# Attention and two mixture layers in one kernel: unit 1's decay summed by VectorE in the keys' tile, remainders of the head on GpSimd, fillers, bank and a load re-placed

## The chip, the cores and the metric

One core of a Trainium2 chip runs the whole program. The metric is the device time of one execution in microseconds (us), taken as the median of several runs; a profile is one further execution. TensorE (PE in rows) does the matmuls, VectorE (DVE), ScalarE (ACT) and GpSimd (POOL) the rest; SyncE (SP) only issues DMAs, and ScalarE and GpSimd issue DMAs of their own as well.

## The reference

Inputs are float32; w_in and w_out reach the kernel as float64, and are converted on the chip.

```python
# B, H, S, D = 2, 8, 576, 64
scores = (1 / sqrt(D)) * matmul(q, k.transpose(0, 1, 3, 2))
cum = cumsum(maximum(s, 0), axis=-1)
bias = -(cum[:, :, :, None] - cum[:, :, None, :])
scores = where(causal, -1e9, scores + minimum(bias, 0))
attn = exp(scores - max(scores)); attn /= attn.sum(-1) + 1e-9
x = matmul(attn, v)                      # -> 1152 tokens x 512
h = x @ w_in; x = maximum(0.01 * h, h) @ w_out          # d_ff 2048
p = domain_probs / domain_probs.sum(-1)                 # 4 experts
out = sum(p[:, e] * (maximum(x @ w1[e], 0) @ w2[e]) for e in range(4))
```

## The kernel before

The work on attention is cut into units. A unit is two heads of one batch over a stretch of tokens: units 0 to 7 are the first 256 tokens (two query tiles i = 1, 0 of 128, two heads j, so four items each), units 8 to 15 the other 320. The function attention() walks over all items in one list; at step i it does the scores of item i, the exponentials of item i-1, the transposes of item i-3, the products with the values of item i-5 and the unit's finish at i-7, and yields three times. The loop at the foot of the program (`for at_ in range(3*64)`, "the head") drives it, and puts other work between: filler matmuls, sums of the decay, the conversion of weights and, from i=24, the first pieces of the dense layer. The head ends when eight units are done. The order on every engine is the order of this program text (`fixed = True`), nothing is moved by a scheduler. DMAs that SP and ScalarE issue take eight completion counters (DMAHW0 to DMAHW7) in turn, in the order of the program, and an issue waits until the DMA eight places before it on the same counter has landed.

The causal decay enters as an additional row of the keys: row D=64 of the tile k_e[n % 3] (ke in rows) holds cum of the unit's two heads, and q_e (qe) has ones there. For unit 0 VectorE computes that row itself: `own` holds the two rows of s on partition 64, and a scan (TENSOR_TENSOR_SCAN in the trace, SCALAR_TENSOR_TENSOR in the listings of order) writes the sums into ke. For later units the scans of all sixteen heads on partitions 0 to 15 (pos, cum; function sums, first 256 columns and then the rest) are computed, and decay(n) issues a DMA on SP that carries two rows of cum into ke. For units 8 and up the float32 keys come again into kd, 288 KB, by a DMA that GpSimd issues, and the rows from cum_d in DRAM.

A score tile is a matmul (ps_sc) that VectorE masks and reduces in one operation (z, mn); ScalarE takes the exponential, TensorE transposes (ps_pt), ScalarE copies (pv), TensorE multiplies with the values (ps_o). Each unit of units 0 to 7 takes the one buffer of ps_o, 256 of 512 columns; VectorE divides by the row sums out of it (xo), TensorE transposes (ps_x).

Weights: fetch64(n) has ScalarE issue a load of 1024 KB of float64 (r); supply() turns it into a float32 tile raw in five steps (one on ScalarE, four on VectorE), has ScalarE store it, issue the next load, round it (w, first half) and another engine compute the remainder `w lo` = raw - w (second half). CONVERTING names the steps i at which supply() goes one step on; from i=31 on it does so in every step. idling(n) is n matmuls that write to the bank `nothing`, read by no one; they stand in each step between the transposes and the products. A float32 matmul is two records in the trace, so that one filler is "x2" there and a single row in a listing of the order.

Of the kernel before, what the change touches and what calls it, by code (L numbers as in the profile page):

```python
# [9 lines left out]
F32 = mybir.dt.float32  # L10
F32R = mybir.dt.float32r
# [8 lines left out]
def attention_moe_moe2(ctx: ExitStack, tc: tile.TileContext, q, k, v, s, w_in, w_out, probs, w1, w2, out):  # L20
# [54 lines left out]
    def f32(ap):  # L75
        return ap.bitcast(F32)
# [35 lines left out]
    def fetch64(n):  # L112
        src, (rows, _) = stream[n][:2]
        r64 = r64p.tile([P, 1024, 2], U32, tag="r64", name="r64")
        r64s.append(r64)
        nc.scalar.dma_start(r64.rearrange("p (a b) t -> p a (b t)", a=rows), src)
# [113 lines left out]
    def split_steps(raw, shape):  # L230

        w = wpool.tile([P, 2, 1024], F32R, tag="w", name="w")
        nc.scalar.copy(w[:, 0], raw)
        yield
        (nc.vector if fixed else nc.gpsimd).tensor_tensor(w[:, 1], raw, f32(w[:, 0]), ALU.subtract)
        yield w.rearrange("p l (a b) -> p l a b", a=shape[0])

    def up_piece(e, f, c):
# [283 lines left out]
    def cumulative():  # L522


        nonlocal cum, idle
        pos, zero, cum = (early.tile([BH, S], F32, name=n) for n in ("pos", "zero", "cum"))
        cum2, own = early.tile([BH, 2, S], F32R, name="cum2"), early.tile([P, 2, half[0]], F32, name="own")[D : D + 1]
        idle = early.tile([P, half[0]], F32, name="idle")

        def sums(lo, hi):  # L530
            part = slice(lo, hi)
            nc.vector.tensor_scalar(pos[:, part], pos[:, part], 0.0, D ** 0.5, ALU.max, ALU.mult)
            nc.vector.tensor_tensor_scan(cum[:, part], pos[:, part], zero[:, part], cum[:, lo - 1 : lo] if lo else 0.0, ALU.add, ALU.add)

        nc.sync.dma_start(own, s[:2, : half[0]])
        nc.scalar.dma_start(pos, s)
        nc.vector.memset(idle, 0.0)
        nc.vector.memset(zero, 0.0)
        idling(8)
        load_keys(0, nc.scalar)  # L540
        load_keys(1, nc.scalar)
        nc.vector.tensor_scalar(own, own, 0.0, D ** 0.5, ALU.max, ALU.mult)
        for j in range(2):
            nc.vector.tensor_tensor_scan(k_e[0][D : D + 1, j], own[:, j], idle[D : D + 1], 0.0, ALU.add, ALU.add)
        load_values(0, nc.scalar)
        fetch64(0)
        sums(0, half[0])
        decay(1, k_e[1])
        load_values(1)
        yield  # L550
        sums(half[0], S)
        yield
        nc.scalar.copy(cum2[:, 0], cum)
        yield
        nc.vector.tensor_tensor(cum2[:, 1], cum, f32(cum2[:, 0]), ALU.subtract)
        nc.sync.dma_start(cum_d.rearrange("l h k -> h l k"), f32(cum2))
        yield
# [104 lines left out]
    class Unit:  # L662
# [3 lines left out]
        def __init__(self, n):  # L666
            b, hp, i0, i1 = self.of = of_unit(n)
            self.items = [(i, j) for i in reversed(range(i0, i1)) for j in range(2)]
            self.ks, self.kd, self.qs = k_split.pop(n) if i0 else (None, k_e[n % 3], q_e[n % 3])
            self.vs = v_s[n % 4]  # L670
            self.z, self.mn, self.pv = {}, {}, {}
            self.o = self.xo = self.rest = None

# [25 lines left out]
        def transposes(self, i, j):  # L699
            z = self.z.pop((i, j))  # L700
            pv = self.pv[i, j] = ap.tile([P, QT, P], F32, tag="pv", name="pv", bufs=4)[:, : i + 1]
            for k0 in range(0, i + 1, 4):
# [3 lines left out]
                    nc.tensor.transpose(pt[:, (kt - k0) * P : (kt - k0 + 1) * P], z[:, tiles[kt][0] : tiles[kt][2]], ident)  # L706
                nc.scalar.copy(pv[:, k0:k1].rearrange("p t q -> p (t q)"), pt)

        def values(self, i, j):
            b, hp, i0, i1 = self.of  # L710
            if self.o is None:
                self.o = ps_o.tile([P, 512], F32, tag="o", name="ps_o")[:, : (i1 - i0) * (2 * D + 2)].rearrange("p (t c) -> p t c", t=i1 - i0)
            pv, cols = self.pv.pop((i, j)), slice(j * (D + 1), (j + 1) * (D + 1))
            for kt in range(i + 1):
                nc.tensor.matmul(self.o[:, i - i0, cols], pv[:, kt], self.vs[:, kt, cols], start=(kt == 0), stop=(kt == i))
            if (i, j) == (i0, 1):
                st = ap.tile([P, i1 - i0, 2, 1], F32, tag="st", name="st")
                sums = self.o[:, :, 0 :: 2 * D + 1].rearrange("p t (h c) -> p t h c", c=1)
                nc.vector.tensor_scalar(st, sums, 1e-9, None, ALU.add)
                nc.vector.reciprocal(st, st)  # L720
                self.xo = ap.tile([P, i1 - i0, 2, D], F32, tag="xo", name="xo", bufs=2)
                o = self.o[:, :, 1 : 2 * D + 1].rearrange("p t (h c) -> p t h c", h=2)
                nc.vector.tensor_tensor(self.xo, o, st.to_broadcast([P, i1 - i0, 2, D]), ALU.mult)

        def finish(self, i, j):

            nonlocal done
            b, hp, i0, i1 = self.of
            if (i, j) != (i0, 1):
                return  # L730
            base, q0, q1 = tiles[i0][:2] + tiles[i1 - 1][2:]
            x = ps_t.tile([P, 512], F32, tag="pt", name="ps_x")[:, : q1 - base]
            for i in reversed(range(i0, i1)):
                nc.tensor.transpose(x[:, tiles[i][0] - base : tiles[i][2] - base], self.xo[:, i - i0].rearrange("p h c -> p (h c)"), ident)
            c = int(i0 > 0)
            dst = slice(b * half[c], (b + 1) * half[c])
            if c == 0:
                nc.scalar.copy(x_t[0][:, 0, hp, dst], x)
                self.rest = x, hp, dst
            else:  # L740
                nc.scalar.copy(x_t[1][:, hp, dst], x)
                done += 1
# [5 lines left out]
                nc.vector.tensor_tensor(x_t[0][:, 1, hp, dst], x, f32(x_t[0][:, 0, hp, dst]), ALU.subtract)  # L748
                done += 1

    done = 0
    ending = False


# [2 lines left out]
    def attention():  # L757

        nonlocal ending
        items, starts, n = [], {}, 0  # L760
        i, split = 0, iter(())
        while n < units or i < len(items) + 8:
            if n < units and i == len(items):
                u = Unit(n)
                starts[n] = i
                items += [(u, *of) for of in u.items]
                if n + 2 < units and not 0 <= n + 2 - 2 * NP < 2:
                    load_keys(n + 2)
                    if n + 2 < 2 * NP:
                        decay(n + 2, k_e[(n + 2) % 3])  # L770
                if n in (2 * NP - 4, 2 * NP - 2):
                    load_keys(n + 4 if n == 2 * NP - 4 else n + 3)
                n += 1
            if n < units - 1 and i == starts[n - 1] + 2:
                load_values(n + 1)
            if i == starts[n - 1] and 2 * NP <= n < units:
                split = split_keys(n)
            for step, lag in STEPS:
                if 0 <= i - lag < len(items):
                    u, *of = items[i - lag]  # L780
                    step(u, *of)
                if lag == 1:
                    next(split, None)
                if lag in (1, 3, 7):

                    late = i - 5 + (lag == 7)
                    ending = lag != 3 and 0 <= late < len(items) and items[late][1:] == items[late][0].items[-1]
                    yield i
            i += 1
# [9 lines left out]
    with ExitStack() as phase:  # L799
# [3 lines left out]

        OPENED = (24, 25, 26, 27, 28, 29, 31, 33, 35)

        CONVERTING = (*range(5, 16), *range(17, 31, 2))
        side, units_of_w, late, opened = attention(), supply(), late_splits(), 0
        nothing = ps_mm.tile([P, 512], F32, tag="mm", name="nothing")
        with tc.tile_pool(name="early", bufs=1) as early:
            ones = pads(early)  # L810
            sums = cumulative()
            next(sums)
            main = mlps(phases[0])

            for at_ in range(3 * 64):
                i = next(side)
                if done == 2 * NP and at_ % 3 == 2:
                    break
                if at_ % 3 == 0 and i in (6, 8):
                    nc.scalar.copy(q_s[i // 2 - 3][D:DK, 1], ones[D:DK])  # L820
                if at_ % 3 == 1:
                    if i < 18:
                        idling(2 if i < 6 else 1)
                    elif opened < len(OPENED) and i >= OPENED[opened] and opened < 3 * (done // 2):
                        next(main)
                        opened += 1
                if at_ % 3 < 2 and i >= 31:
                    onto_held()
                if at_ % 3 == 2:
                    if i == 3:  # L830
                        fetch64(1)
                    if i in (3, 4, 5):
                        next(sums)
                    if i in CONVERTING or i >= 31:
                        next(units_of_w)
        hidden_pool(phase, 6)
# [92 lines left out]
```

## Time and profile before

| | |
|---|---|
| median of 3 runs | 726.74 us (726.07 to 726.77) |
| the profiled execution's own time | 725.75 us |
| its span, first to last instruction | 723.9 us (1.85 us of the time lie around it) |
| busy: TensorE, VectorE, ScalarE, GpSimd | 707.4, 442.2, 322.4, 253.6 us |
| granted TensorE clock, mean | 0.999 |
| bytes moved by DMA | 70.68 MB |
| instructions | 11398 |

Busy times are sums over the whole span; in the first 60 us the engines share the work differently from later, so the rows below are read by stretch. One difference between two kernels is the difference of their medians; the profiled execution lies 0.99 us below the median.

### The profile page before, as it was taken

The page shows a single profiled execution, that of the slowest core. Times are in us where ns is not written, and L with a number is a line of the kernel's source. Part 1 is how long each engine was busy: PE and PEld are TensorE (multiplying, and loading weights), DVE is VectorE, ACT ScalarE, POOL GpSimd, SP SyncE. Part 2 cuts the span into 40 slices and gives each one's busy share as a digit, 9 for nine tenths or more (in the row PEclk, how much of TensorE's full clock was granted, in tenths as well). Part 3 has the DMA queues.
Part 4 walks back from the last instruction along what each step waited for, and adds up shares of the span by engine and source line. Part 5 has one row for each costly group of instructions (what it writes and reads, how often), then busy time and mean ns, then how long its engine had stood idle before and what let it go on. Part 6 is the DMA issues. An engine that isn't in the chain of part 4 may idle for free.

```text
span 723.9 us, 11398 instructions
## 1 busy us (share of the span) xinstructions
PE 707.4 (98%) x4376; PEld 644.8 (89%) x4376; DVE 442.2 (61%) x893; ACT 322.4 (45%) x642; POOL 253.6 (35%) x226
## 2 busy tenths in 40 slices
PE   8899999999999999999999999999999999999998
PEld 7678889888878999999988989889889898898986
DVE  6778897998679656844943644545346344364452
ACT  5667877876735755634432322314224133232210
POOL 5000000000028789883372442704625227142200
PEclk9999999999999999999999999999999999999999
DMA  8966868575452222221120302101111021020002
GB/s 220 238 190 170 233 177 249 174 239 211 159 184 88 86 90 88 73 75 59 39 79 1 88 30 59 59 1 59 58 32 56 30 59 59 0 59 1 1 35 97
DMA packets 41878, 70.68 MB, mean 98 GB/s; under 512 B 4112, under 2 KB 23328, under 8 KB 41824
## 3 DMA queue, kind: packets, MB, share of 16 engines
q1 hardware_dynamic: 31296, 41.87, 19.6%
q10 hardware_dynamic: 9376, 25.73, 10.6%
q0 software_dynamic: 1152, 2.36, 1.6%
q8 instruction: 34, 0.56, 0.3%
q14 instruction: 20, 0.16, 0.1%
HBM read 59.11 MB, written 10.82 MB: 97 GB/s over the span
## 4 chain that ended last, share of the span: by engine, by line
PE 91%; DVE 3%; ACT 2%; DMA 2%; issue 1%; ACTq 0%; DVEq 0%; SPq 0%
PE ps_d L43 41%; PE ps_u L43 36%; PE ps_o L43 6%; PE ps_sc L43 4%; PE ps_pt L43 3%; DMA r<-in_moe_w_in_dram 1%; DMA ke<-in_k_dram 1%; PE nothing L43 1%; DVE t L43 1%; ACT z L43 1%; ACT w L43 0%; DVE w L43 0%; PE ps_x L43 0%; ACT pv L43 0%; DVE z L43 0%
## 5 line engine op out<-in xcount | busy, mean ns | idle before, releaser
L43 PE MATMUL ps_u<-t,w 128*128 128x320 f32 (+1 forms) x1680 | 236.5, 299 | 1.2 <-DVE t L43 1.2
L43 PEld LDWEIGHTS ps_u<-t,w 128*128 128x128 f32 x1680 | 233.0, 189 | 4.8 <-DVE t L43 1.4
L43 PE MATMUL ps_d<-w,ht 128*128 128x512 f32 (+1 forms) x876 | 203.4, 388 | 0.0
L43 PEld LDWEIGHTS ps_d<-w,ht 128*128 128x128 f32 x876 | 160.9, 188 | 31.5
L43 POOL TENSOR_TENSOR w<-raw,w 128x512 fp32r<-128x512 f32 (+2 forms) x72 | 109.1, 1535 | 218.6 <-ACT w L43 218.5
L43 ACT ACTIVATE ht<-ps_u 128x320 fp32r<-128x320 f32 (+2 forms) x176 | 74.2, 432 | 161.9 <-DVE ps_u L43 129.3
L43 DVE SCALAR_TENSOR_TENSOR oacc<-ps_d,pn,oacc 128x512 f32<-128x512 f32 (+1 forms) x64 | 47.5, 743 | 104.0 <-PE ps_d L43 104.0
L43 PE MATMUL ps_d<-ht,w 128*128 128x320 f32 (+1 forms) x576 | 109.5, 340 | 1.3 <-DVE y L43 1.3
L43 ACT CAST w<-raw 128x1024 fp32r<-128x1024 f32 (+2 forms) x88 | 63.9, 757 | 82.4 <-PE ps_d L43 76.4
L43 PEld LDWEIGHTS ps_d<-ht,w 128*128 128x128 f32 x576 | 90.9, 188 | 7.2 <-issue 1.7
L43 PEld LDWEIGHTS ps_o<-vs,pv 128*128 128x128 f32 x480 | 63.1, 191 | 8.7 <-issue 3.8
L43 DVE SCALAR_TENSOR_TENSOR ht<-ps_u,ht 128x320 fp32r<-128x320 f32 (+1 forms) x128 | 56.4, 453 | 23.3 <-ACT ht L43 22.0
L43 DVE TENSOR_TENSOR ps_u<-ps_u,tmp 128x320 f32<-128x320 f32 (+1 forms) x120 | 56.2, 471 | 23.5 <-PE ps_u L43 21.9
L43 PE MATMUL ps_o<-vs,pv 128*128 128x65 f32 x480 | 62.9, 267 | 3.0 <-issue 1.3
L43 POOL TENSOR_TENSOR w<-sums,w 128x1024 fp32r<-128x1024 f32 x24 | 58.7, 2445 | 8.0 <-ACT w L43 8.0
L43 DVE TENSOR_TENSOR tmp<-ps_u,tmp 128x320 f32<-128x320 f32 (+1 forms) x80 | 36.9, 464 | 39.7 <-PE ps_u L43 38.7
L43 POOL TENSOR_TENSOR sums<-raw 128x256 f32<-128x256 f32 x48 | 37.3, 797 | 58.9 <-DVE sums L43 57.4
L43 PE MATMUL ps_u<-x,w 128*128 128x512 f32 x192 | 56.6, 411 | 0.9 <-DVE x L43 0.9
L43 ACT ACTIVATE z<-z,mn 128x256 f32<-128x256 f32 (+4 forms) x80 | 48.5, 607 | 20.0 <-DVE mn L43 13.6
L43 POOL DMA_DIRECT2D kd<-in_k_dram x8 | 5.1, 638 | 140.6 <-PE ps_sc L43 140.6
L43 DVE CUSTOM_DVE_ANT_0 z<-ps_sc,mask 128x256 f32<-128x256 f32 (+4 forms) x80 | 41.0, 513 | 15.4 <-PE ps_sc L43 12.1
L43 ACT COPY pv<-ps_pt 128x512 f32<-128x512 f32 (+3 forms) x96 | 38.9, 422 | 14.1 <-PE ps_pt L43 13.7
(77 smaller groups left out, 657.2 us busy)
## 6 DMA issues: line engine op xcount, KB each, us to landing
raw<-in_moe_w_dram SPq DMA_DIRECT2D x32, 512.0 KB, 3.5
raw<-w_f SPq DMA_DIRECT2D x24, 512.0 KB, 3.9
r<-in_moe_w_in_dram ACTq DMA_DIRECT2D x8, 1024.0 KB, 6.3
w_f<-raw ACTq DMA_DIRECT2D x16, 512.0 KB, 3.8
r<-in_moe_w_out_dram ACTq DMA_DIRECT2D x8, 1024.0 KB, 7.6
qr<-in_q_dram SPq DMA_DIRECT2D x16, 160.0 KB, 7.6
kd<-in_k_dram POOLq DMA_DIRECT2D x8, 288.0 KB, 6.3
kr<-in_k_dram SPq DMA_DIRECT2D x8, 288.0 KB, 3.6
```

The lines of the kernel that those rows point to most:

```text
L43: ins = call(*args, **kw)
```

## The change

Five things are edited. Unit 1 gets its decay like unit 0: `own` has four rows, a second DMA brings the s of unit 1, and VectorE scans them into k_e[1] between the first score tiles; the decay DMA of unit 1 goes, that of unit 2 is issued behind the key loads of unit 3, and the common sums are computed later. In the head the remainders of the weights are computed by GpSimd. Units 0 to 7 share one ps_o buffer, even units in its last columns and odd ones in its first, with the tiles' places mirrored in odd ones. The second float64 load is issued at i=4 in place of 3. The table CONVERTING and the fillers are re-placed: two fillers in steps 12 to 23 (before, one in 12 to 17 and none in 18 to 23).

```diff
-        (nc.vector if fixed else nc.gpsimd).tensor_tensor(w[:, 1], raw, f32(w[:, 0]), ALU.subtract)
+        (nc.vector if fixed and not heading else nc.gpsimd).tensor_tensor(w[:, 1], raw, f32(w[:, 0]), ALU.subtract)
...
-        nc.sync.dma_start(own, s[:2, : half[0]])
+        for n in range(2):
+            nc.sync.dma_start(own[:, 2 * n : 2 * n + 2], s[n * H : n * H + 2, : half[0]])
...
-        for j in range(2):
-            nc.vector.tensor_tensor_scan(k_e[0][D : D + 1, j], own[:, j], idle[D : D + 1], 0.0, ALU.add, ALU.add)
         load_values(0, nc.scalar)
         fetch64(0)
+        load_values(1)
+        for j in range(4):
+            nc.vector.tensor_tensor_scan(k_e[j // 2][D : D + 1, j % 2], own[:, j], idle[D : D + 1], 0.0, ALU.add, ALU.add)
+            if j > 0:
+                yield
         sums(0, half[0])
-        decay(1, k_e[1])
-        load_values(1)
         yield
...
+        def slot(self, i):
+            i0, i1 = self.of[2:]
+            return i - i0 if i0 > 0 or self.even else i1 - 1 - i
...
+                    if shared_o is None:
+                        shared_o = ps_o.tile([P, 512], F32, tag="o", name="ps_o")
+                    o = shared_o[:, 512 - n :] if self.even else shared_o[:, :n]
...
                     load_keys(n + 2)
-                    if n + 2 < 2 * NP:
-                        decay(n + 2, k_e[(n + 2) % 3])
+
+                    for m in () if n == 0 else (2, 3) if n == 1 else range(n + 2, min(n + 3, 2 * NP)):
+                        decay(m, k_e[m % 3])
...
-        CONVERTING = (*range(5, 16), *range(17, 31, 2))
+        CONVERTING = (*range(5, 10), *range(12, 22), *range(23, 31, 2))
...
-                    if i < 18:
-                        idling(2 if i < 6 else 1)
+                    if i < 24:
+                        idling(2 if i < 6 or i >= 12 else 1)
...
-                    if i == 3:
+                    if i == 4:
                         fetch64(1)
-                    if i in (3, 4, 5):
-                        next(sums)
+                    if i < 7:
+                        next(sums, None)
```

VectorE at the start of the program, the difference of the two orders (ISA z,mn is the masking operation of one score tile, ISA mn the read of its minimum; ke_113 is the keys' tile of unit 0, ke_115 that of unit 1):

```order
-L43 TENSOR_SCALAR own<-own 1x512
+L43 TENSOR_SCALAR own<-own 1x1024
 L43 SCALAR_TENSOR_TENSOR ke_113<-own,idle 1x256 x2
+L43 ISA z,mn<-ps_sc,mask 128x256
+L43 ISA mn 128x1
+L43 SCALAR_TENSOR_TENSOR ke_115<-own,idle 1x256
+L43 ISA z,mn<-ps_sc,mask 128x256
+L43 ISA mn 128x1
+L43 SCALAR_TENSOR_TENSOR ke_115<-own,idle 1x256
+L43 ISA z,mn<-ps_sc,mask 128x128
+L43 ISA mn 128x1
 L43 TENSOR_SCALAR pos<-pos 16x256
```

The two scans of unit 1 now stand behind the first and second score tile of unit 0, and the first half of the common sums behind the third in place of ahead of the first.

SP behind the first key loads, the difference of the two orders with the semaphores that each row waits for (ke_117 and qe_116 are unit 2's keys and queries, ke_113 and qe_112 in this place unit 3's, vs values):

```order
 L43 DMA qe_116<-in_q_dram 64x2x256 [waits DMAHW3_49]
-L43 DMA ke_117<-cum 1x2x256 [waits DMAHW5_49,Pool_49]
-L43 DMA vs<-in_v_dram 128x2x128 [waits DMAHW6_49,Pool_49]
-L43 DMA ke_113<-in_k_dram 64x2x256 [waits DMAHW7_49,PE_49]
-L43 DMA qe_112<-in_q_dram 64x2x256 [waits DMAHW0_49]
+L43 DMA vs<-in_v_dram 128x2x128 [waits DMAHW4_49,Pool_49]
+L43 DMA ke_113<-in_k_dram 64x2x256 [waits DMAHW5_49,PE_49]
+L43 DMA qe_112<-in_q_dram 64x2x256 [waits DMAHW6_49]
+L43 DMA ke_117<-cum 1x2x256 [waits DMAHW0_49,DVE_49]
 L43 DMA ke_113<-cum 1x2x256 [waits DMAHW1_49]
```

The decay row of unit 2 moved from ahead of the loads of unit 3 to behind them, and the counters that these loads wait for are others.

TensorE in unit 3, the difference of the two orders with waits (ke_113 is unit 3's keys here):

```order
 L43 MATMUL ps_pt<-ident,z 128x128 [waits DVE_49,PE_49]
 L43 MATMUL ps_pt<-ident,z 128x128
-L43 MATMUL nothing<-idle 128x128
+L43 MATMUL nothing<-idle 128x128 x2
 L43 MATMUL ps_o<-vs,pv 128x65
 L43 MATMUL ps_sc<-ke_113,qe_112 128x256
 L43 MATMUL ps_pt<-ident,z 128x128 [waits Activation_49]
-L43 MATMUL nothing<-idle 128x128
-L43 MATMUL ps_o<-vs,pv 128x65 [waits DVE_49,DMAHW6_49,PE_49,Pool_49]
+L43 MATMUL nothing<-idle 128x128 x2
+L43 MATMUL ps_o<-vs,pv 128x65 [waits DMAHW4_49,DVE_49,Pool_49]
```

A second filler stands in each step, and the first product of the unit lost its wait for TensorE and kept the one for VectorE. On GpSimd the order is now two remainders of the head, the two kd loads of units 8 and 9, the third remainder; before, the kd loads stood first and no remainder was there. On ScalarE the second float64 load stands one exponential and one copy further back, and takes another completion counter (7 in place of 4).

## Rows read from the trace of the kernel before

**Rows 1.** Windows: stretch, its us, each engine's busy us (instructions), clock, DMA share, GB/s.

```profile
5.10:21.50 16.40, 13.48 (x98) 12.17 (x98) 11.15 (x37) 12.65 (x27) 5.47 (x14) 1.00 1.08 252
21.50:37.40 15.90, 13.48 (x96) 11.39 (x97) 11.50 (x41) 11.16 (x29) 0.00 (x0) 1.00 0.95 254
...
60.00:190.00 130.00, 128.00 (x858) 114.06 (x858) 109.93 (x223) 96.58 (x170) 3.77 (x6) 1.00 0.67 206
```

**Rows 2.** Timeline to 14 us: start, us, engine, operation, out<-in, idle before and releaser.

```profile
0.75 0.75 SPq L43 DMA_DIRECT2D own<-in_s_dram  x1
...
3.33 1.31 DVE L43 TENSOR_TENSOR_SCAN ke<-own,idle 1x256 f32<-1x256 f32 x2
...
4.67 0.45 DVE L43 TENSOR_SCALAR pos<-pos 16x256 f32<-16x256 f32 x1
...
6.33 0.43 DVE L43 CUSTOM_DVE_ANT_0 z<-ps_sc,mask 128x256 f32<-128x256 f32 x1 [0.50 <-POOL vs L43]
...
8.43 0.29 DVE L43 CUSTOM_DVE_ANT_0 z<-ps_sc,mask 128x128 f32<-128x128 f32 x1 [0.37 <-PE ps_sc L43]
...
10.51 0.67 PE L43 MATMUL ps_sc<-ke,qe 128*128 128x256 f32 x2 [1.46 <-DMA ke<-cum]
...
11.12 1.02 SPq L43 DMA_DIRECT2D qe<-in_q_dram  x1
...
11.33 0.42 DVE L43 CUSTOM_DVE_ANT_0 z<-ps_sc,mask 128x256 f32<-128x256 f32 x1 [1.47 <-PE ps_sc L43]
...
12.43 0.42 DVE L43 CUSTOM_DVE_ANT_0 z<-ps_sc,mask 128x256 f32<-128x256 f32 x1 [0.67 <-PE ps_pt L43]
```

**Rows 3.** Timeline, 14 to 40 us: units 2 and 3.

```profile
15.02 0.67 PE L43 MATMUL ps_sc<-ke,qe 128*128 128x256 f32 x2
...
21.53 0.65 SPq L43 DMA_DIRECT2D ke<-in_k_dram  x1
21.56 0.67 PE L43 MATMUL ps_sc<-ke,qe 128*128 128x256 f32 x2 [1.33 <-issue]
...
23.32 1.04 ACT L43 CAST w<-raw 128x1024 fp32r<-128x1024 f32 x1 [2.11 <-DMA ke<-in_k_dram]
```

**Rows 4.** The chain of waits, 0 to 160 us: start, us, what.

```profile
8.65 8.70 DMA r<-in_moe_w_in_dram
```

**Rows 5.** The tile kd up to 60 us: its loads' way, issue to landing.

```profile
DMA to landing us min/median/max: 9.3/10.0/10.7
```

**Rows 6.** Timeline of TensorE alone, 26 to 40 us.

```profile
27.44 0.65 PE L43 MATMUL ps_sc<-ke,qe 128*128 128x256 f32 x2
...
28.15 0.39 PE L43 MATMUL nothing<-idle 128*128 128x128 f32 x2
28.37 0.34 PE L43 MATMUL ps_o<-vs,pv 128*128 128x65 f32 x2
28.54 0.65 PE L43 MATMUL ps_sc<-ke,qe 128*128 128x256 f32 x2
...
30.90 0.44 PE L43 MATMUL ps_sc<-ke,qe 128*128 128x128 f32 x2
...
32.52 0.65 PE L43 MATMUL ps_sc<-ke,qe 128*128 128x256 f32 x2
```

**Rows 7.** Groups by form: GpSimd (whole run), VectorE (to 62 us): busy, mean ns.

```profile
L43 POOL TENSOR_TENSOR w<-raw,w 128x1024 fp32r<-128x1024 f32 x24 | 59.9, 2513 | 149.3 <-ACT w L43 149.2
...
L43 DVE TENSOR_TENSOR w<-raw,w 128x1024 fp32r<-128x1024 f32 x3 | 3.7, 1222 | 0.7 <-ACT w L43 0.7
```

**Rows 8.** Timelines of GpSimd and of VectorE around 221 us.

```profile
221.03 2.63 POOL L43 TENSOR_TENSOR w<-sums,w 128x1024 fp32r<-128x1024 f32 x1 [2.75 <-ACT w L43]
...
221.32 3.43 DVE L43 TENSOR_TENSOR w<-raw,w 128x1024 fp32r<-128x1024 f32 x1
```

**Rows 9.** Timeline, 40 to 75 us: end of the head.

```profile
50.96 0.19 PEld L43 LDWEIGHTS ps_sc<-kd,qs 66*128 66x128 f32 x1
...
52.29 0.37 ACT L43 COPY pv<-ps_pt 128x256 f32<-128x256 f32 x1 [1.38 <-PE ps_pt L43]
```

More of the change, by code (lines that the diff above doesn't have):

```diff
@@ L526, in cumulative @@
         pos, zero, cum = (early.tile([BH, S], F32, name=n) for n in ("pos", "zero", "cum"))
-        cum2, own = early.tile([BH, 2, S], F32R, name="cum2"), early.tile([P, 2, half[0]], F32, name="own")[D : D + 1]
+        cum2, own = early.tile([BH, 2, S], F32R, name="cum2"), early.tile([P, 4, half[0]], F32, name="own")[D : D + 1]
         idle = early.tile([P, half[0]], F32, name="idle")
@@ L669, in __init__ @@
             self.ks, self.kd, self.qs = k_split.pop(n) if i0 else (None, k_e[n % 3], q_e[n % 3])
-            self.vs = v_s[n % 4]
+            self.vs, self.even = v_s[n % 4], n % 2 == 0
             self.z, self.mn, self.pv = {}, {}, {}
@@ L707, in transposes @@
                 nc.scalar.copy(pv[:, k0:k1].rearrange("p t q -> p (t q)"), pt)
+        def slot(self, i):
+            i0, i1 = self.of[2:]
+            return i - i0 if i0 > 0 or self.even else i1 - 1 - i
         def values(self, i, j):
+            nonlocal shared_o
             b, hp, i0, i1 = self.of
             if self.o is None:
-                self.o = ps_o.tile([P, 512], F32, tag="o", name="ps_o")[:, : (i1 - i0) * (2 * D + 2)].rearrange("p (t c) -> p t c", t=i1 - i0)
-            pv, cols = self.pv.pop((i, j)), slice(j * (D + 1), (j + 1) * (D + 1))
+                n = (i1 - i0) * (2 * D + 2)
+                if i0 > 0:
+                    o = ps_o.tile([P, 512], F32, tag="o", name="ps_o")[:, :n]
+                else:
+                    if shared_o is None:
+                        shared_o = ps_o.tile([P, 512], F32, tag="o", name="ps_o")
+                    o = shared_o[:, 512 - n :] if self.even else shared_o[:, :n]
+                self.o = o.rearrange("p (t c) -> p t c", t=i1 - i0)
+            pv, cols, slot = self.pv.pop((i, j)), slice(j * (D + 1), (j + 1) * (D + 1)), self.slot(i)
             for kt in range(i + 1):
-                nc.tensor.matmul(self.o[:, i - i0, cols], pv[:, kt], self.vs[:, kt, cols], start=(kt == 0), stop=(kt == i))
+                nc.tensor.matmul(self.o[:, slot, cols], pv[:, kt], self.vs[:, kt, cols], start=(kt == 0), stop=(kt == i))
             if (i, j) == (i0, 1):
@@ L733, in finish @@
             for i in reversed(range(i0, i1)):
-                nc.tensor.transpose(x[:, tiles[i][0] - base : tiles[i][2] - base], self.xo[:, i - i0].rearrange("p h c -> p (h c)"), ident)
+                nc.tensor.transpose(x[:, tiles[i][0] - base : tiles[i][2] - base], self.xo[:, self.slot(i)].rearrange("p h c -> p (h c)"), ident)
             c = int(i0 > 0)
@@ L749, in second_term @@
                 done += 1
-    done = 0
+    done, shared_o = 0, None
     ending = False
```

## Prediction, made before the changed kernel ran

> **What bounds the kernel now.** I read the table by engine and stretch first [rows 1]. From 60 to 190 us TensorE works 128.00 of 130.00 us at granted clock 1.00, the 2.4 GHz level, and the stretches ahead show 1.00 too. So two things hold. What the head saves or loses before 60 us moves the end by as much, because nothing behind it has slack that could swallow it. And filler matmuls can win no clock here, since none is missing. All that the change touches lies in the head, the first 60 us, where TensorE is idle 2.92 us of 16.40 up to 21.5 us and 2.42 of 15.90 in the units 3, 4 and 5 (21.50 to 37.40); one unit is two heads' first 256 tokens, four score tiles. In these stretches no engine is full, and the sixteen transfer engines are (share 1.08 and 0.95): the head waits now for a transfer, now for a chain that passes through all of them.
>
> The timeline gives the waits. TensorE waits 1.46 us at 10.51 for the decay row of unit 1, which a DMA carries from cum to the keys' tile, and VectorE starves behind it, 1.47 before 11.33 [rows 2]. It waits 1.33 us at 21.56 for unit 3; the page can't name the releaser ("issue"), but SP's queue goes on at 21.53, 0.03 us before, and both wait for one thing: the q load of unit 3, issued at 11.12, has to land [rows 2, 3]. The chain of waits shows what is slow there: the second float64 load of 1024 KB, issued at 8.65, takes 8.70 us [rows 4], and the two kd loads, issued by GpSimd for units 8 and 9, take 9.3 to 10.7 us in the same stretch [rows 5].
>
> **The change part by part.** *Unit 1's decay on VectorE.* A second own load stands on SP ahead of the k load of unit 0 and delays it by one issue, 0.75 us; z of the first tile goes from 6.33 to 7.08. From there VectorE alone carries the start: z 0.43, scan 0.65 (1.31 for two), z 0.43, scan 0.65, z 0.29, the half sum 0.45 and a scan of 0.65: the z of the fourth tile starts at 10.63 where it started at 8.43 [rows 2], 2.2 late. (The first operation on own has twice the elements, too; it ends before the k load has landed.) The 1.47 idle ahead of 11.33 takes up all but 0.7 of this, and the idle 0.67 ahead of the next z at 12.43 nearly all the rest. So TensorE's 1.46 wait goes, and VectorE's own chain takes its place with hardly the same length: I count +0.3 at unit 2, between +0.1 (both gaps taken) and +0.7 (only the first). The gain that is left if VectorE's chain is shorter than I think is 1.46−0.75 = 0.7; that is the bound on the other side.
>
> *Unit 3's wait.* The kd loads (0.58 MB, worth 2.3 us of the 252 GB/s of this stretch, [rows 1]) go behind GpSimd's two remainders, to about 37 us; the second float64 load goes one exponential and one copy later on ScalarE; the q load of unit 3 has one transfer fewer ahead of it on SP. I take the 1.33 wait as gone. With the +0.3 the start and unit 3 give −1.0, between −0.6 (0.7 is left) and −2.0 (1.33 and 0.7 both gained). The price of the new order on SP: the decay row of unit 2 is issued behind unit 3's keys and queries. I estimate that it lands at 14.3 to 15.5; its score starts at 15.02 now and would start at about 15.3. This is the cover that can fail (second rival).
>
> *18 more fillers.* One filler takes 0.22 us of TensorE (28.15 to 28.37), so 4.0 us are added in units 3 to 5. What hides them? A unit's own matmuls, read where no wait stands between: 27.44 to 28.54 is 1.10 with a filler, 0.88 without; the step from 28.54 has the same score and about as much behind it, and I take 0.94; the last two steps, 30.90 to 32.52, have neither filler nor wait and take 1.62 [rows 6]. That makes 3.44, and with eight fillers (two in each of four steps) 3.44+1.76 = 5.2. The three units take 15.9 now (5.9, 5.1 and 4.9: 21.56, 27.44, 32.52 and the stretch's end, [rows 1, 3, 6]), so each has over a microsecond of waits for VectorE and ScalarE, and the fillers fall into these: 15.6 if nothing else waits. If all waits stayed it would be 13.48+3.96+2.42 = 19.9, and if the fillers only stood in the idle time that they find, 13.48+3.96 = 17.4; the first I exclude, since a filler stands behind a transpose and ahead of matmuls that wait anyway. I take 16.1, a fifth of the idle time kept: +0.2, between −0.3 and +1.5. The 2.11 us that ScalarE idles before the cast of w at 23.32 [rows 3] hang on a transfer counter that SP's k load of unit 4 holds until it lands, and this load itself stood behind the float64 load; after the change both wait for earlier ones. This speaks for the lower half.
>
> *Remainders on GpSimd.* VectorE loses three operations of 1.22, GpSimd gets three of 2.51 [rows 7], on an engine with nothing to do there; the reader of a remainder is a matmul several steps later. But the two engines stop each other: the VectorE remainder at 221.32 took 3.43 us, not 1.22, while GpSimd's of 221.03 ran for 2.63 [rows 8]. So a VectorE operation with two tiles of 1024 columns, or one of the conversion, that starts just behind GpSimd's can lose up to 2.21. The z operations read PSUM and one tile; no row shows whether they are held. I take +0.4 for all three: only the first stands where VectorE is on the path (the start of unit 4), and there for about half of the 1.1 that is left of GpSimd's operation on average. Bounds 0 and +2.2.
>
> The Trainium skill ("SBUF — State Buffer", section "Who interferes with whom") says that VectorE and GpSimd share a pair of ports under an exclusive lock: a VectorE instruction with two SBUF inputs contends with a GpSimd one that reads SBUF, and the later one blocks until the first has ended. The 3.43 of this trace agrees. By that rule in full the sum would hold 2.2 in place of the 0.4.
>
> *The end of the head.* Conversions stand one step earlier from step 31 on, and VectorE has fewer of the remainders. ScalarE's copy at 52.29 waits 1.38 for transposes [rows 9], and what is ready sooner there can fill it; kd is first read at 50.96 [rows 9] and its load, by my estimate issued at 37 to 38.4 and under way for at most the 9.3 to 10.7 of now [rows 5], lands at 49 at the latest: hidden, and only 2 us of cover. I take −0.5, between 0 and −1.4.
>
> *The shared bank.* Its first product in each unit no longer waits for TensorE, but still for VectorE, which in the order is the division of the unit before. So it costs and gives nothing.
>
> **Sum.** −1.0+0.2+0.4−0.5 = −0.9 on the profiled execution's 725.75: 724.85. The median of the runs shown is 726.74, 0.99 above that execution, so I forecast −0.9 there too: 725.8.
>
> **The rivals.**
> A, faster: VectorE's chain is short enough that both waits of the start are saved, −2.0, the fillers all stand in waits (0), and the lock bites little (0): with −0.5 it is −2.5, 724.2. For it: the 0.67 and 1.47 of idle, and the 15.6. Against: VectorE has 11.15 busy us of 16.40 in this stretch [rows 1], and all of the start's scans are in series.
> B, slower: the decay row of unit 2, now last on SP behind unit 3's loads with the transfer engines full, lands late, and TensorE waits at unit 2 in place of unit 1 and 3. It costs what it is later than 15.0; the whole is slower by 1.45 from a landing at about 17.5. At 18.5 (issued at about 11, and under way for a little less than the 8.70 of the float64 load of this stretch [rows 4]) it is +3.5−1.33+0.6−0.5 = +2.3: 729.0. For it: the q load of unit 3, which now stands ahead of it, needed from 11.12 to 21.5. Against: it is a row of 2 KB, and the 0.58 MB of kd are out of its way.
> C: the lock in full, first remainder 2.2 and not 0.4: −0.9+1.8 = +0.9, 727.6.
> That the shared bank does nothing is in the forecast.
>
> **How the numbers follow.** A difference of 0.2%, 1.45 us, is about what a measurement of this kernel can tell from no change. Forecast 0.50 (its own range 724.9 to 726.6), A 0.28, B 0.11, C 0.11. Faster by over 1.45: A, and a fifth of the forecast's spread, 0.38. Slower: B, and a little of C, 0.13. The rest, 0.49, is the same. For 8 in 10 the range reaches from the better half of A, 723.9, to C, 727.6.
>
> **What the profile after would show.** Right: no wait of TensorE for a DMA of cum at unit 1, z of the fourth tile at 10.4 to 10.9 with VectorE busy without a gap from 7 to 12; unit 3's first score without "issue", at about 20.5; units 3 to 5 in 15.6 to 16.6 with 17.4 busy or a little less; the three GpSimd operations of 2.5 in the head and a VectorE conversion of over 1.5 beside one; kd issued at 37 to 38. Wrong: a TensorE wait of over 1 us for cum at unit 2 (B); VectorE operations of 3 us beside each remainder, with TensorE idle behind (C); units 3 to 5 in 17 or more, the fillers in the way; a first score at 50.96 that waits for kd; or the start ending where it did with both waits gone (A).

## The result, and the profile after

The changed kernel takes 732.03 us (median of 4 runs, 731.41 to 734.51) against 726.40 of the kernel before (725.38 to 726.77): ratio 1.0083, 95% interval 1.0059 to 1.0107. It is 5.6 us slower where 0.9 faster was forecast. When the same kernel was measured again (r1 below), on 12 executions, it was 730.16 against 727.51: 1.0045, 1.0020 to 1.0069. One of all executions here, of 739.28 us in e3, fell in a slow state and is left out.

The page of the changed kernel begins so:

```profile
span 730.3 us, 11480 instructions
```

The same windows as in [rows 1], and below them the stretch in which TensorE's clock (the figure after GpSimd's busy time) fell, in the changed kernel's profile:

```profile
5.10:21.50 16.40, 13.24 (x86) 12.21 (x86) 11.50 (x34) 10.23 (x21) 4.25 (x13) 1.00 0.76 224
21.50:37.40 15.90, 15.63 (x124) 14.20 (x123) 12.68 (x43) 10.78 (x28) 2.36 (x1) 1.00 0.72 182
37.40:50.90 13.50, 11.83 (x72) 10.51 (x72) 6.06 (x21) 7.46 (x22) 3.62 (x3) 0.87 1.12 262
60.00:190.00 130.00, 126.36 (x852) 112.73 (x850) 111.69 (x227) 98.20 (x173) 6.34 (x7) 1.00 0.69 216
...
38.00:40.00 2.00, 0.90 (x9) 0.76 (x7) 0.30 (x2) 1.09 (x2) 0.00 (x0) 1.00 1.04 353
41.00:42.00 1.00, 1.00 (x8) 0.91 (x7) 0.62 (x4) 0.88 (x4) 1.00 (x1) 0.63 0.93 340
43.00:44.00 1.00, 1.00 (x5) 0.71 (x4) 0.09 (x1) 0.00 (x0) 0.65 (x2) 0.50 1.07 349
```

From 21.5 to 37.4 TensorE is now busy 15.63 of 15.90: the fillers did fill its idle time, and the kernel was no faster for it. The losses are in the other rows: 3.16 us idle up to 21.5 with 12 instructions fewer done, and a stretch around 42 in which the clock is at 0.50, the 1.2 GHz level, after TensorE had been busy 0.90 of the 2 us from 38 on.

Where the time went is read best from the start of each unit's first score. In the changed kernel's two profiles (the first, and r1's) against the kernel before, in us:

| first score of unit | 0 | 1 | 2 | 3 | 6 | 8 | 9 | 11 | end of the span |
|---|---|---|---|---|---|---|---|---|---|
| before | 5.09 | 10.51 | 15.02 | 21.56 | 37.42 | 50.88 | 64.1 | 101.8 | 723.9 |
| changed, first profile | 6.32 | 11.75 | 18.11 | 23.16 | 42.71 | 57.12 | 71.9 | 108.4 | 730.3 |
| changed, r1 | 6.10 | 9.69 | 15.47 | 20.51 | 37.36 | 50.83 | 68.4 | 104.9 | 727.8 |

The same program takes two courses. In the first it loses 6.24 us up to unit 8; in r1 nothing up to there, and 4.3 between units 8 and 9 (17.58 in place of 13.24; the first profile loses 1.6 there). The timeline of the first profile shows how the early course goes:

```profile
4.20 0.68 DVE L43 TENSOR_SCALAR own<-own 1x1024 f32<-1x1024 f32 x1 [2.46 <-DMA own<-in_s_dram]
6.32 1.19 PE L43 MATMUL ps_sc<-ke,qe 128*128 128x256 f32 x2 [1.34 <-DVE ke L43]
7.31 1.06 PE L43 MATMUL nothing<-idle 128*128 128x128 f32 x4
11.28 0.59 SPq L43 DMA_DIRECT2D ke<-in_k_dram  x1
12.61 0.37 ACTq L43 DMA_DIRECT2D r<-in_moe_w_in_dram  x1
12.62 1.30 SPq L43 DMA_DIRECT2D ke<-cum  x2
18.11 0.67 PE L43 MATMUL ps_sc<-ke,qe 128*128 128x256 f32 x2 [1.83 <-DMA vs<-in_v_dram]
...
38.43 0.43 ACTq L43 DMA_DIRECT2D r<-in_moe_w_out_dram  x1
38.91 1.04 ACT L43 CAST w<-raw 128x1024 fp32r<-128x1024 f32 x1 [1.23 <-DMA qr<-in_q_dram]
40.57 0.44 PE L43 MATMUL ps_x<-ident,xo 128*128 128x128 f32 x2 [1.67 <-ACT pv L43]
42.71 1.16 PE L43 MATMUL ps_sc<-ke,qe 128*128 128x256 f32 x2
```

TensorE idles 1.34 us ahead of the first score, because own now waits for the second load of s, and then runs at half its pace (two fillers in 1.06 us, 0.61 elsewhere) until about 10.5. The windows print a clock of 1.00 there, but this is no reading: the trace's records of the granted clock begin only at 10.54 us in this profile, at 5.01 in r1 and at 5.94 in the kernel before, and the windows take a stretch without a record for full clock. In all fourteen profiles filler records that follow each other start 0.21 us apart ahead of the first record of the clock and 0.11 behind it, so TensorE starts every one of them at the lower of its two levels. So unit 0's last score starts at 10.86 (8.01 before), and the key load of unit 3, which overwrites unit 0's keys, leaves SP at 11.28, not 9.1 as in r1. The decay row of unit 2 is behind it and leaves at 12.62, in the same moment as the second float64 load of 1024 KB; in r1 it leaves at 10.68, 0.21 us ahead of that load. Unit 2 starts at 18.11 and not at 15.47: of these 2.64 us the row's later issue is 1.94. The conversion slips too, the third float64 load leaves at 25.85 (23.20 in r1) and holds ScalarE until 35.98, with unit 8's q load beside it, and the chain of waits shows what that does:

```profile
31.02 7.39 DMA qr<-in_q_dram
38.41 0.02 issue
38.43 0.43 ACTq L43
```

ScalarE's issue of the fourth float64 load waits for that q load, whose counter it shares; the copies behind it come late, TensorE starves, and its clock falls to 0.5 from 41.3 to 44.7.

In r1 (timeline) the late course:

```profile
6.10 0.67 PE L43 MATMUL ps_sc<-ke,qe 128*128 128x256 f32 x2 [1.12 <-DMA ke<-in_k_dram]
6.61 0.61 PE L43 MATMUL nothing<-idle 128*128 128x128 f32 x4
10.68 1.29 SPq L43 DMA_DIRECT2D ke<-cum  x2
10.89 0.37 ACTq L43 DMA_DIRECT2D r<-in_moe_w_in_dram  x1
15.47 0.67 PE L43 MATMUL ps_sc<-ke,qe 128*128 128x256 f32 x2 [0.99 <-DVE mn L43]
...
26.14 1.65 DVE L43 TENSOR_SCALAR raw<-raw 128x1024 f32<-128x1024 f32 x1
...
54.27 2.36 POOL L43 TENSOR_TENSOR w<-raw,w 128x1024 fp32r<-128x1024 f32 x1 [15.42 <-ACT w L43]
54.37 2.94 DVE L43 TENSOR_TENSOR qs<-qr,qs 64x640 fp32r<-64x640 f32 x1
60.50 0.45 PE L43 MATMUL ps_pt<-ident,z 128*128 128x128 f32 x1 [2.81 <-DVE x L43]
```

The same operation on qs in the kernel before and in e8, with GpSimd idle:

```profile
54.92 0.81 DVE L43 TENSOR_TENSOR qs<-qr,qs 64x640 fp32r<-64x640 f32 x1
58.59 0.81 DVE L43 TENSOR_TENSOR qs<-qr,qs 64x640 fp32r<-64x640 f32 x1
```

The third remainder starts on GpSimd 0.1 us before VectorE's operation on qs, and this takes 2.94 us where it takes 0.81 with GpSimd idle. VectorE is late with all that follows, TensorE waits 2.81 us for x, and the clock falls, as r1's windows show:

```profile
56.00:59.00 3.00, 1.69 (x14) 1.37 (x12) 2.96 (x5) 2.24 (x6) 0.63 (x1) 1.00 1.02 377
59.00:62.00 3.00, 1.50 (x4) 1.27 (x5) 2.80 (x6) 1.09 (x3) 0.00 (x0) 0.60 0.55 138
62.00:65.00 3.00, 3.00 (x14) 2.97 (x13) 0.57 (x2) 0.00 (x0) 0.00 (x0) 0.50 0.37 98
65.00:68.00 3.00, 3.00 (x23) 3.00 (x21) 1.93 (x5) 1.85 (x4) 0.62 (x1) 0.76 0.01 3
```

### The profile page after: what moved, and what is told of

Its sections match the earlier page's. It is cut to its first block, busy times and chain, and to the rows that moved or that the text cites. A ratio compares the mean times of both kernels' runs of the same rounds, so it can differ in the third digit from the quotient of the medians.

```text
span 730.3 us, 11480 instructions
## 1 busy us (share of the span) xinstructions
PE 713.3 (98%) x4412; PEld 651.6 (89%) x4412; DVE 442.4 (61%) x892; ACT 322.9 (44%) x642; POOL 260.8 (36%) x229
## 4 chain that ended last, share of the span: by engine, by line
PE 88%; DVE 4%; DMA 3%; ACT 2%; issue 2%; SPq 0%; ACTq 0%; DVEq 0%
PE ps_d L43 40%; PE ps_u L43 35%; PE ps_o L43 5%; PE ps_sc L43 3%; PE ps_pt L43 3%; DMA qr<-in_q_dram 1%; PE nothing L43 1%; DVE z L43 1%; DMA w_f<-raw 1%; DVE t L43 1%; DMA raw<-w_f 1%; ACT z L43 1%; ACT raw L43 0%; DVE raw L43 0%; SPq L43 0%
## 5 line engine op out<-in xcount | busy, mean ns | idle before, releaser
L43 POOL TENSOR_TENSOR w<-raw,w 128x256 fp32r<-128x256 f32 (+2 forms) x75 | 115.8, 1562 | 263.4 <-ACT w L43 245.6
L43 POOL TENSOR_TENSOR sums<-raw 128x256 f32<-128x256 f32 x48 | 37.3, 796 | 57.2 <-DVE y L43 55.7
L43 PE MATMUL ps_pt<-ident,z 128*128 128x128 f32 x240 | 40.3, 276 | 3.3 <-DVE x L43 2.8
```

Of the source, the lines that this page charges most:

```text
L43: ins = call(*args, **kw)
```

## The experiments

Edits are against the changed kernel unless another is named. The kernel before ran beside them; single executions of it lay between 724.5 and 732.2 us, so the medians (of 10 or 12 runs, 6 in e11) and their intervals count, and the starts in the profiles, one of each, more. e1 to e4 ran on another chip than r1 and all that follows it, so their times are compared with the kernel before, not with r1.

**e1, the fourth float64 load later.**

```diff
-            if len(r64s) < CONVERTED:
+            if len(r64s) < CONVERTED and not (heading and len(r64s) == 3):
...
+                    if i == 24:
+                        fetch64(3)
```

> The changed kernel, but the fourth float64 load (the first of w_out) is issued at step 24, not behind the store at step 20. Theory T (transfers): at 38.4 us ScalarE stands behind this issue, whose counter is held by unit 8's q load until it lands, TensorE starves 1.67 us and its granted clock falls to 0.5 until 44.6; without it unit 6 and unit 7 come about 3 to 4 us earlier: 728 to 729, no stretch at clock 0.5. Rival F (the 18 fillers and the port lock cost the time by themselves): unit 6 stays near 42.7, time 731 to 732. Rival S (the late start pushes everything): the same as F, 731 to 732.

729.08 against 726.65: 1.0023 (0.9998 to 1.0049). Unit 6 started at 37.30 and unit 8 at 50.77 with no drop of the clock before 70. That is nearly the forecast of T (728 to 729), but its profile had also fallen into the quick start (unit 1 at 9.78, unit 2 at 14.99), so it doesn't prove the load alone; it brought the question of the start.

**e2, the fillers of before.**

```diff
-                    if i < 24:
-                        idling(2 if i < 6 or i >= 12 else 1)
+                    if i < 18:
+                        idling(2 if i < 6 else 1)
```

> The changed kernel with the fillers of before (18 fewer). Theory T: units 3 to 5 are up to 0.5 us each shorter, but ScalarE then waits the longer for the same transfer, so unit 6 starts at 41.5 to 42.7 and the time is 731 to 732. Rival F: the fillers' 4.0 us come back in large part, 728 to 729. Rival S: 731 to 732.

732.62: 1.0063 (1.0037 to 1.0088). Units 3 and 4 took 5.31 and 5.19 us in place of 5.73 and 5.71, and ScalarE's wait took that back: TensorE waited 1.70 behind it, at 39.34. The fillers are not where the time went; F falls. T had the wait and the time about right, but unit 6, at 40.34, came earlier than its 41.5 to 42.7.

**e3, the conversion steps of before** (the old CONVERTING).

> The changed kernel with the conversion steps of before (5 to 15, 17, 19 ..). Theory T: the third float64 load is issued two steps earlier (about 22 in place of 25.9 us) and is off the wires before unit 8's loads; but now the store of step 21 has its counter behind the same q load: unit 6's wait is shorter, not surely gone, 728 to 731. Rival F and rival S: no change beyond 1 us, 731 to 733.

730.76 (the median of nine): 1.0048 (1.0020 to 1.0077), which doesn't tell T from F and S. With a quick start unit 8 was at 51.80, so no gain over r1 (50.83). And from unit 9 to unit 11 it took 37.7 us like the kernel before (64.1 to 101.8), as do e9 and e11, which have the old steps too (37.7, 37.9); with the new steps it is 36.5 in the changed kernel and in most of the others (37.3 and 37.5 in e6 and e2). So a gain of up to 1.2 us in this stretch comes with the new conversion steps.

**e4, unit 1's decay by DMA again** (own, decay and sums as in the kernel before).

> The changed kernel with unit 1's decay by DMA again, own with two rows, the decay of unit 2 ahead of unit 3's loads. Theory T: first score at 5.1 in place of 6.3 and unit 2 without its 1.83 wait, unit 1 with 1.46 again; the later stall of unit 6 hangs on a transfer and stays, so 729.5 to 731.5. Rival S: all that follows is early by the 1.2 of the start and the 1.8 of unit 2 and the collisions vanish, 726 to 727. Rival F: 729 to 730, units 3 to 5 still 5.7 each.

729.65: 1.0022 (0.9994 to 1.0051). First score at 5.15, no wait at unit 2 (14.92), unit 8 at 51.34. So without this part the early losses are gone, and what was left is the wait for x, 2.82 us at 61.02, and a clock of 0.50 behind it. S falls with the time; F's 729 to 730 is met, too, but e2 speaks against F. The stall of unit 6 that T expected to stay had shrunk, to 0.48 us of TensorE at 36.43, so T's time came out, but not by that stall.

**r1, the changed kernel again, e5 with 11 fillers at the start, e6 with these and e1's late load, e7 with the second load of s moved.** e5 and e7:

```diff
-        idling(8)
+        idling(11)
```

```diff
-        for n in range(2):
-            nc.sync.dma_start(own[:, 2 * n : 2 * n + 2], s[n * H : n * H + 2, : half[0]])
+        nc.sync.dma_start(own[:, :2], s[:2, : half[0]])
...
         load_keys(1, nc.scalar)
+        nc.sync.dma_start(own[:, 2:], s[H : H + 2, : half[0]])
-        nc.vector.tensor_scalar(own, own, 0.0, D ** 0.5, ALU.max, ALU.mult)
+        nc.vector.tensor_scalar(own[:, :2], own[:, :2], 0.0, D ** 0.5, ALU.max, ALU.mult)
...
         for j in range(4):
+            if j == 2:
+                nc.vector.tensor_scalar(own[:, 2:], own[:, 2:], 0.0, D ** 0.5, ALU.max, ALU.mult)
```

(e7 also has e1's edit.)

> The changed kernel once more, as the measure for the three beside it. Theory P (TensorE's pace at the start): TensorE idles 1.3 us between its first 16 filler records and the first score at 6.3, and it is left to the execution whether its pace doubles ahead of this gap or only at about 10.4; so executions fall in two groups, some 2 to 4 us apart, and a profile has unit 1's first score at 9.8 or at 11.7, unit 2's at 15.0 or at 18.1. Rival D (the decay row's place on SP alone): unit 2's first score is at 18 in every profile, executions in one group, 731.5 to 733.

> The changed kernel with 11 in place of 8 fillers ahead of the first score, so that TensorE has no gap there. Theory P: the fillers of step 0 take 0.22 each, not 0.43, unit 1 at 9.8, unit 2 at 15.0 to 15.3 with a wait under 0.7; unit 6's stall is shorter, as all of ScalarE's loads go out 1 to 2 us earlier; 727 to 729.5. Rival D: unit 2 at 17.5 to 18.1 with 1.8 of wait, 731 to 732.5. Rival F (fillers only cost): 0.4 worse than the changed kernel.

> Eleven fillers at the start, and the fourth float64 load at step 24. Theory P with theory T: unit 2 at 15.0 to 15.3, no wait of ScalarE for the q load, unit 6 at 37.0 to 37.6 as before the change, 726 to 727.5, within 0.2% of the kernel before, and with a smaller spread than the first run with the late load (726.8 to 732.1). Rival D: 729 to 730.

> The fourth float64 load at step 24, and the second load of s behind the key loads on SP, with the operation on own cut in two, so that unit 0 waits for no more than before (8 fillers). Theory P: the first score is at 5.1 again with no gap on TensorE, pace full from about 6.5 as in the kernel before; unit 1 at 9 to 10, unit 2 at 14 to 15; 725 to 727. If the start's 1.2 us were passed on to the end in full whatever the pace is, it would be 1.2 below the run with both; if it is taken up by later waits, the same.

Measured: r1 730.16, e5 730.97 (1.0051, 1.0027 to 1.0075), e6 729.33 (1.0018, 0.9993 to 1.0043), e7 730.27 (1.0036, 1.0012 to 1.0060). The starts went as P said (unit 1 at 9.67 to 9.78, unit 2 at 14.45 to 15.47, in e7 the first score at 4.95), and D falls with r1, which is the same program as the first profile and had unit 2 at 15.47. That the times fall in two groups is not shown. ScalarE's wait for the q load is not bound to the slow start: e5 has it with the quick one (TensorE 1.59 us at 38.07, unit 6 at 39.52). With e1's edit it is in none of four profiles (e1, e6, e7, e10: unit 6 at 37.18 to 37.92); without it it is in the first profile, e2, e5 and e8 (1.01 to 1.40 us), shorter in e4 (0.72), and not in r1; in e3 ScalarE waits 1.16 there, and the trace can't name for what. So T's part is shown. But the times did not follow, and the forecasts of e5, e6 and e7 all missed, by 1.5 to 3.3 us: all four profiles have the wait of 2.8 us for x. Something behind unit 8 cost as much as the start.

**e8, the third remainder on VectorE; e9, the kernel before with the three remainders on GpSimd; e10, e7's edits with e8's.** e8, and e9 against the kernel before:

```diff
-        (nc.vector if fixed and not heading else nc.gpsimd).tensor_tensor(w[:, 1], raw, f32(w[:, 0]), ALU.subtract)
+        (nc.vector if fixed and not (heading and len(ready) < 2) else nc.gpsimd).tensor_tensor(w[:, 1], raw, f32(w[:, 0]), ALU.subtract)
```

```diff
-        (nc.vector if fixed else nc.gpsimd).tensor_tensor(w[:, 1], raw, f32(w[:, 0]), ALU.subtract)
+        (nc.vector if fixed and not heading else nc.gpsimd).tensor_tensor(w[:, 1], raw, f32(w[:, 0]), ALU.subtract)
```

> The changed kernel with the third remainder of the head on VectorE again, the first two on GpSimd. Theory L (port lock): VectorE's qs operation of 64x640 at about 54 takes 0.8 in place of 2.94, TensorE has no wait of 2.8 us for x at about 60, and the granted clock stays at 1.00 from 50 to 70; from unit 8's first score to the end it takes 673 us as in the kernel before (677 in the changed kernel's second profile), so 2 to 3.5 us less in executions that had the drop: median 728 to 729. Rival P (only the start's pace and the q load matter): the same as the changed kernel beside it, 730 to 731.

> The kernel before with the three remainders on GpSimd and nothing else changed. Theory L: a VectorE operation of 2 to 3 us beside the third remainder, a wait of TensorE of 1 us or more behind it at 58 to 61, and in a part of the executions a granted clock of 0.5 for 3 to 7 us: 1.5 to 3.5 us slower than the kernel before. Rival P: no more than 0.5 slower.

> The changed kernel with all three mends: second load of s behind the key loads with own cut in two, the fourth float64 load at step 24, the third remainder on VectorE. Theories P, T and L together: first score at 5.0, unit 2 at 15.0, unit 8 at 50.6, no drop of the clock up to 70, 673 us from there: 1 to 0 below the kernel before in its fast executions, 725.5 to 727.5. If the waits only move on, 728 to 730.

| | median | ratio to before, interval | unit 8 | to unit 9 | runs with a mean clock of 0.999 or more |
|---|---|---|---|---|---|
| before, beside r1 | 727.51 | | 50.88 | 13.2 | 13 of 35 |
| before, beside e8, e9 and e10 | 727.23 | | 50.88 | 13.2 | 12 of 28 |
| changed (r1) | 730.16 | 1.0045 (1.0020 to 1.0069) | 50.83 | 17.6 | 1 of 12 |
| e8 | 728.46 | 1.0014 (0.9994 to 1.0035) | 55.05 | 12.7 | 7 of 12 |
| e9 | 728.90 | 1.0039 (1.0017 to 1.0061) | 50.57 | 16.2 | 1 of 12 |
| e10 | 725.14 | 0.9976 (0.9951 to 1.0001) | 51.39 | 12.7 | 9 of 12 |

(The units are those of the profiles; the kernel before has a single one. In the profiles a mean clock below 0.999 goes with a fall to 0.5 for 3.4 us or more.) The timeline of e9, which has nothing of the change but the remainders, shows the same three steps:

```profile
55.90 2.38 POOL L43 TENSOR_TENSOR w<-raw,w 128x1024 fp32r<-128x1024 f32 x1 [16.13 <-ACT w L43]
56.37 2.52 DVE L43 TENSOR_TENSOR ks<-kr,ks 64x576 fp32r<-64x576 f32 x1
60.11 0.45 PE L43 MATMUL ps_pt<-ident,z 128*128 128x128 f32 x1 [2.18 <-DVE x L43]
```

and its windows the clock behind them:

```profile
59.00:62.00 3.00, 1.89 (x6) 1.64 (x7) 2.40 (x5) 0.89 (x2) 0.00 (x0) 0.67 0.79 238
62.00:65.00 3.00, 3.00 (x21) 3.00 (x20) 0.89 (x4) 0.81 (x3) 0.00 (x0) 0.76 0.42 110
```

In e8 the operation on qs is 0.81 us again, and its windows have no drop:

```profile
59.00:62.00 3.00, 2.92 (x22) 2.50 (x21) 2.96 (x6) 3.00 (x8) 0.00 (x0) 1.00 1.00 348
62.00:65.00 3.00, 2.35 (x17) 2.23 (x18) 2.94 (x6) 1.58 (x4) 0.00 (x0) 1.00 0.93 269
```

So L is shown from both sides: with the third remainder taken back, the wait of 2.8 us goes and 1.7 us of the median with it; with the remainders added alone, the wait comes, with 1.7 us. Two more comparisons bear it out. e10 differs from e7 by this one line, and takes 725.14 in place of 730.27, with intervals that don't meet. And over all fourteen profiles the way from unit 8 to unit 9 takes 12.7 to 13.2 us with the third remainder on VectorE (four profiles) and 14.8 to 17.6 with it on GpSimd (ten). e8's profile had the slow start (units 1 and 2 at 11.68 and 17.95, unit 6 at 41.59), which e10 mends as well. e10 is the fastest kernel of the study, 2.1 us below the kernel before, though its interval just touches no difference. Most of that goes with the clock: among executions with a mean clock of 0.999 or more it takes 724.96 and the kernel before 725.40, but 9 of 12 are such in e10 and 12 of 28 in the kernel before.

**e11, the kernel before with unit 1's decay alone, in e7's form.**

> The kernel before with unit 1's decay by VectorE alone, in the mended form (second load of s behind the keys, own cut in two); remainders, fillers, conversion steps, float64 loads as before. Theory: unit 1 at 9.7 in place of 10.5, unit 3 without its 1.33 wait only if the kd loads were not what held its q load; as kd stays early here, unit 3 at 20.5 to 21.5. Then units 4 to 8 0.3 to 1 us earlier than before: 725.5 to 727. If the second float64 load is what holds it and it moves by nothing, 727.

734.26: 1.0094 (1.0066 to 1.0122), a clear miss. Its timeline:

```profile
9.62 0.37 ACTq L43 DMA_DIRECT2D r<-in_moe_w_in_dram  x1
9.68 1.33 POOL L43 DMA_DIRECT2D kd<-in_k_dram  x2
10.68 1.30 SPq L43 DMA_DIRECT2D ke<-cum  x2
19.38 1.19 PE L43 MATMUL ps_sc<-ke,qe 128*128 128x256 f32 x2 [4.83 <-issue]
```

The decay row of unit 2 leaves 1.06 us after the second float64 load and 1.00 after the first kd load, and TensorE waits 4.83 us at unit 2; the clock falls to 0.5 at 18 to 24. In the changed kernel, where the float64 load and kd leave later, unit 2 waits 1.83 us at most; so the change's parts hang together here. Which of the two loads holds the row in e11 was not tried.

## Why the prediction was wrong, step by step

Two steps failed. The remainders' +0.4 was put at the wrong one of the three; this is the loss of r1 and a part of the first profile's. And the start's +0.3 left out the clock and the sum had no term for the fourth float64 load; these are most of the first profile's loss.

- **Remainders on GpSimd, +0.4.** This term failed most: the step said that only the first remainder stands where VectorE is on the path. Measured on VectorE in r1: 1.65 in place of 0.69 at the first, which cost no wait, and 2.94 in place of 0.81 at the third. The third lies at the head's end, where VectorE was busy for 8.38 of 9.10 us already before the change, as this window of the kernel before shows:

```profile
50.90:60.00 9.10, 8.19 (x57) 7.14 (x57) 8.38 (x22) 7.28 (x15) 0.00 (x0) 1.00 0.76 245
```

  The wait for x that it makes costs 1.6 us between units 8 and 9 where the clock doesn't fall (the first profile, e1 and e6: 14.8) and 3.0 to 4.3 where it does (the other seven). Rival C had the mechanism, and put it at the wrong remainder.
- **The fourth float64 load, no term.** The step on the fillers saw ScalarE held by a transfer counter at 23.32 and took that as gone; it didn't ask about the next such issue, and the sum has nothing for it. In the first profile ScalarE stood 1.23 us behind a counter that unit 8's q load held, TensorE 1.67, and the clock fell; from unit 3 to unit 8 it took 33.96 us, 30.32 in e1, which moves this load, and 29.32 in the kernel before.
- **What a wait costs.** The working took a wait of TensorE at its length. Two of them here, of 1.67 us in the first profile and of 2.81 in r1, had a clock of 0.5 at their end; others, such as 2.81 in the first profile and 2.82 in e1 and e6, had none, so it is a matter of the execution. That the fillers can win no clock was said because the clock read 1.00 throughout. That was true of the one profiled execution behind its first 5.94 us, not of the kernel: 16 of the 28 executions of the kernel before beside e8 to e10 have a mean clock under 0.999, and their median is 728.1 against 725.4 of the rest. With the third remainder on GpSimd the falls are more frequent (11 of 12 executions in r1 and in e9). What makes the clock fall in the kernel before is not shown; its profile has no fall but in the last 1.2 us.
- **Unit 1's decay, +0.3 at unit 2.** In r1 0.45, by the mechanism that was worked out: the z of the fourth tile starts at 10.58 (10.63 forecast), and unit 2 waits for VectorE. In the first profile 3.09: the lower clock behind the gap at the start was not foreseen, nor that the second load of s delays own itself, to 4.20.
- **The decay row of unit 2.** The step estimated 14.3 to 15.5 for its landing. Its landing has no record of its own. Unit 2 starts at 15.47, where it waits for VectorE, or at 18.11, past rival B's limit of 17.5. From the row's issue to that score it is 4.79 us in r1 and 3.79 in e5, where TensorE doesn't wait for it, 5.49 in the first profile and 8.70 in e11. The row left 0.21 us ahead of the second float64 load in r1 and e5, together with it in the first profile, and 1.06 behind it in e11, there with kd in front of it as well. This fits a row that the large loads hold up, but isn't shown apart from the rest: of the first profile's 2.64 us against r1, 1.94 are that the row left later.
- **Unit 3's wait, with the start −1.0.** Right in r1: unit 3 at 20.51 against 21.56, and no wait. In the first profile it came 1.60 late, with unit 2. e9, which keeps the start of before, has unit 3 at 20.17 without the wait, so the remainders on GpSimd, with kd behind them, can take it away alone. The kd loads left at 37.52 in r1, as estimated, and nothing waited for them.
- **18 fillers, +0.2.** Units 3 to 5 take 16.85 us in r1, not 16.1, against 15.86: +1.0. e2 gives 0.4 to 0.5 a unit for the fillers. The bounds held, the size didn't. But the three units take 16.94 in e9 as well, which has the remainders on GpSimd and no added filler: there the first remainder held a VectorE operation for 2.86 us (0.69 otherwise), so here, too, the lock has a price that the step didn't see.
- **The end of the head, −0.5.** In e8 and e10 unit 8 to 9 takes 0.5 less than before, and units 9 to 11 another 1.1 less.
- **The shared bank, 0.** Nothing shows otherwise; it wasn't tried alone.

r1 sums up as −1.05 up to unit 3, +1.0 in units 3 to 5, 0 to unit 8, +4.3 to unit 9, −1.2 to unit 11, +0.8 behind: +3.9 on the span. The first profile is +6.24 to unit 8, +1.6, −1.2, −0.3: +6.35. Open is what sends an execution down the one course or the other. It is the moment at which the clock rises: 10.5 to 10.6 us in the three profiles with the slow start (the first, e2, e8), 4.1 to 6.8 in the other eleven. The fillers ahead of the gap look the same in the first profile and in r1 (16 records in 3.78 us). Where TensorE idles 1.1 us or more ahead of the first score (the first profile, r1, e1, e2, e3, e8) the start was slow in three of six, elsewhere in none of eight; this speaks for the gap, but doesn't prove it. e5, which closes the gap, had no better median.

## What to carry to other kernels

When work goes to GpSimd, look up what VectorE does with two tiles in SBUF at the moment that GpSimd is let go, for every one of the moved operations, and not only what VectorE is spared. Issue a small row that a matmul needs ahead of a large load, whatever the queue, and check by the issue times, not by the order of one queue. Price a wait of TensorE with what its clock does after it. And look at the clock of all executions, not of the profiled one alone, before saying that none is missing.

## What the runs showed of the hardware

- VectorE beside GpSimd: with two inputs in SBUF, 2.94 for 0.81, 2.52 for 0.75; a TENSOR_SCALAR with one input 1.65 for 0.69, in r1. Each ended 0.55 to 0.68 us behind GpSimd's operation. The Trainium skill ("SBUF — State Buffer", section "Who interferes with whom") says that both kinds can contend, the second kind in a two-port mode; the traces agree that both are held, and no trace shows the mode.
- TensorE starts at the 1.2 GHz level (fillers 0.43 us each, not 0.22), in these profiles up to 4.1 to 6.8 or 10.5 to 10.6 us. The rows print 1.00 there because the trace has no record of the clock yet: the pace is to be read from the durations.
- A q load of 160 KB took 7.39 us from issue to landing beside a load of 1024 KB, and by its completion counter it held up another engine's issue (ScalarE, 1.23 us), in the first profile.
